# Attention scan with an MLP on one core: one sum moved from VectorE to matmuls, mask copies moved from GpSimd, and a new order of steps

## The chip, the cores and the metric

The kernel runs on one core of one Trainium2 chip. The metric is the device time of one execution in microseconds (us), taken outside the profiler; three runs of the kernel before gave 550.18, 550.34 and 550.40 us, median 550.34.

## What is computed

A gated linear attention with a complex decay, and a two-layer MLP on its output. The decay is normalised first; the change touches the magnitude in it.

```python
B, H, S, D = 4, 8, 768, 48
mag = np.sqrt(a_re * a_re + a_im * a_im)
scale = np.minimum(mag, 0.999) / (mag + 1e-06)
a_re_n, a_im_n = (a_re * scale, a_im * scale)
for t in range(S):
    new_re = ar * S_re - ai * S_im
    new_im = ar * S_im + ai * S_re
    S_re, S_im = (new_re + k_t v_t^T, new_im)
    y[t] = q_t @ S_re
...
h = x @ w_in            # 3072 x 384 by 384 x 2048
out = (h * sigmoid(1.702 * h)) @ w_out
```

## The kernel before

The 3072 tokens are cut into 12 units of 256 tokens. A unit has two chunks of 128 tokens, and unit 0 is prepared in two parts of 128 tokens. Units form groups: unit 0 alone, unit 1 alone, then pairs. For each unit three things happen:

- `prepare_part` (L298 on) turns the decay into factors for q and k: squares on ScalarE (L207), their sum on VectorE (`both("sum", ...)`, helper line L231), logarithm, root and reciprocal on ScalarE (L331 to L336), products and scans over time on VectorE (L358, L378, and L398 for the angle), sine and cosine on ScalarE (L421 to L427; L406 turns the angle into a count of turns), the products with q and k on VectorE (L231), and DMAs that rearrange them by head (`remap`, L452 to L456).
- `attend` (L460 on) makes scores on TensorE (L517), masks them on VectorE (L523), transposes keys (L536, copied out as `kt` by ScalarE, L542), sums scores and state into `x_ps` (L507, copied out at L567), and makes the new state in `z_ps` (L561, "state matmuls" below).
- `moe` (L625 on) multiplies by the weights: `h_ps` (L657), the activation on ScalarE (L665, L669, L671), `o_ps` (L686). Group 0 uses the weights whole, in float32; the groups after it use them split in a high and a low part. The weights come as 64-bit floats and are turned to 32-bit ones by three VectorE steps and one ScalarE step for each 768 columns (`convert`: L249, L252, L255, L256).

Each step is put down by `plan.add` with its engine and with keys that it reads and writes. A table of numbers, `ORDER`, then lists all steps; they are issued in that order, so each engine and the SP queue of DMAs run theirs in the table's order, each engine in order of its own queue.

TensorE begins with 20 "filler" matmuls (L434, `WARM = 20`), products with the identity whose result nobody reads. Ahead of the table stand constants: the identity, a causal mask in four rotated forms (one made by memset and affine_select, three more by 12 copies of 32 rows by 128 columns on GpSimd, L160), and zeroed state tiles.

The core of what is edited:

```python
both("sum", u, i, rk("sum"), d, m, d, ALU.add, r=k_mag, w=k_den)
...
add("ACT", a_t(C), rk("root"), lambda: act(out=m, in_=d, func=AF.Ln, bias=b_tiny), r=k_den, w=k_mag, ...)
...
nc.gpsimd.tensor_copy(out=mask[o * QL : (o + 1) * QL, j, :], in_=mask[g * QL : (g + 1) * QL, 0, :])
```

Of the kernel before, what the change touches and what calls it, by code (L numbers as in the profile page):

```python
# [95 lines left out]
def attention_moe(ctx: ExitStack, tc: tile.TileContext, qk_in, v, a_in, w_in, w_out, qn, kn, vn, an, bn, out):  # L96
# [49 lines left out]
    nc.vector.memset(b_hpi, HALF_PI)  # L146
    make_identity(nc, ident)
    nc.gpsimd.memset(mask, 1.0)
    nc.gpsimd.memset(runs, 1)
    run_of = {T: runs[:, 0 : NR * (T + 1)], L: runs[:, NR * (T + 1) :]}  # L150
    for n, x in run_of.items():
        nc.gpsimd.memset(x.rearrange("p (r t) -> p r t", t=n + 1)[:, :, 0], 0)
    nc.gpsimd.affine_select(
        out=mask[:, 0, :], in_=mask[:, 0, :], pattern=[[1, P]], compare_op=ALU.is_ge,
        fill=0.0, base=0, channel_multiplier=-1,
    )
    for j in range(1, 4):
        for g in range(4):
            o = (g + j) % 4
            nc.gpsimd.tensor_copy(out=mask[o * QL : (o + 1) * QL, j, :], in_=mask[g * QL : (g + 1) * QL, 0, :])  # L160
# [65 lines left out]
    def both(op, u, i, rank, out, a, b, alu, **kw):  # L226
        n = 1
        for x in out.shape[1:]:
            n *= x
        e, en, t = two(on(op, u, i), n)  # L230
        add(en, t, rank, lambda: e.tensor_tensor(out=out, in0=a, in1=b, op=alu), **kw)  # L231
# [66 lines left out]
    def prepare_part(u, i, a, b, np_, mag, den, rec, sp, th, *keys):  # L298
# [31 lines left out]
        both("sum", u, i, rk("sum"), d, m, d, ALU.add, r=k_mag, w=k_den)  # L330
        add("ACT", a_t(C), rk("logd"), lambda: act(out=g, in_=m, func=AF.Ln, bias=b_tiny), r=k_mag, w=k_sp, tab=LOGS, grp=u or None)  # L331
        add("ACT", a_t(C) - 0.1, rk("logd"), lambda: act(out=g, in_=g, func=AF.Exp, scale=-0.5), w=k_sp, tab=LOGS, grp=u or None)
        add("ACT", a_t(C), rk("root"), lambda: act(out=m, in_=d, func=AF.Ln, bias=b_tiny), r=k_den, w=k_mag, tab=LOGS, grp=u or None)
# [430 lines left out]
    for g, us in enumerate(GROUPS):  # L764
        for u in us:
            prepare(u)
            attend(u)
        moe(g)
        if g == 0:
            for n in range(2 * NP):  # L770
                split(n)
# [375 lines left out]
```

## Time and profile before

| what | value |
|---|---|
| median of 3 runs | 550.34 us |
| the profiled execution's own time | 550.39 us |
| its span, first to last instruction | 548.7 us |
| TensorE busy | 521.2 us, 95% |
| VectorE busy | 391.1 us, 71% |
| ScalarE busy | 368.7 us, 67% |
| GpSimd busy | 12.3 us, 2% |
| granted TensorE clock | 1.00 |

The profiled execution took 0.05 us more than the median, and 1.69 us of it lie outside the span. Busy shares are averages: VectorE is full in the first fifth of the span and a quarter full at the end, while TensorE starts late and is then busy to the end. In a timeline row "start us, us" is a merged stretch of like instructions, xN their count; a float32 matmul leaves two records. On VectorE and ScalarE the listed time of an instruction is longer than the distance to the next one's start where the two overlap, so what an instruction costs its queue is read from the starts.

### The profile page before, as it was taken

Reading aid. Unit: us, or ns where it says so; the run is one execution under the profiler, and the core shown is the slowest. Engines: PE = TensorE matmul, PEld = TensorE weight load, DVE = VectorE, ACT = ScalarE, POOL = GpSimd, SP = SyncE. Lnnn points to the kernel's source line nnn. Section 1 sums busy time; section 2 is a strip of 40 time slices with the busy share of each in tenths; the row PEclk is TensorE's granted clock in tenths of the full one; section 3 lists DMA queues with packets and bytes.
Section 4 is the critical chain, followed back from the end, with each engine's and each line's share of the span. In section 5 each row is a group of like instructions: output and inputs, shape, how many; then the busy total and the mean of one; then the engine's idle time right before and its main releaser. Section 6 shows DMA issues by size and latency. Waiting matters only on the chain.

```text
span 548.7 us, 14354 instructions
## 1 busy us (share of the span) xinstructions
PE 521.2 (95%) x6122; PEld 446.9 (81%) x6122; DVE 391.1 (71%) x625; ACT 368.7 (67%) x559; POOL 12.3 (2%) x55
## 2 busy tenths in 40 slices
PE   0399999999999999999999999999999999999997
PEld 0389988999988888888888888888888888888885
DVE  7999999999979989987766844856366535421142
ACT  7898989979699988688795679248665242132221
POOL 7000000000000000000000000000000000000000
PEclk9999999999999999999999999999999999999999
DMA  8859963626576668868237427445441162100121
GB/s 344 284 191 354 252 258 89 206 54 156 201 181 202 151 197 206 236 168 252 74 92 228 68 65 174 145 133 117 136 134 49 50 145 91 62 15 34 39 87 61
DMA packets 29253, 82.02 MB, mean 149 GB/s; under 512 B 4096, under 2 KB 7168, under 8 KB 29184
## 3 DMA queue, kind: packets, MB, share of 16 engines
q1 hardware_dynamic: 29184, 81.06, 50.5%
q8 instruction: 49, 0.80, 0.6%
q14 instruction: 20, 0.16, 0.1%
HBM read 57.41 MB, written 4.72 MB: 113 GB/s over the span
## 4 chain that ended last, share of the span: by engine, by line
PE 89%; DVE 8%; DMA 1%; issue 1%; ACT 1%; SPq 0%; DVEq 0%
PE o_ps L686 36%; PE h_ps L657 36%; PE x_ps L507 7%; PE z_ps L561 3%; PE z_ps L517 3%; PE p_ps L517 2%; DVE qk L231 1%; PE p_ps L536 1%; PE z_ps L536 1%; DMA raw<-in_w_in_dram 1%; DVE s L231 1%; DVE valA L256 1%; DVE qr L231 1%; DVE valU L252 0%; DMA qkh<-qk 0%
## 5 line engine op out<-in xcount | busy, mean ns | idle before, releaser
L669 ACT ACTIVATE gh<-h_ps 128x512 fp32r<-128x512 f32 x88 | 52.4, 596 | 108.2 <-PE h_ps L657 76.5
L673 DVE TENSOR_TENSOR gl<-h_ps,gh 128x512 fp32r<-128x512 f32 x88 | 60.3, 687 | 85.3 <-ACT h_ps L671 74.0
L657 PE MATMUL h_ps<-xhi,hiA 128*128 128x512 f32 (+1 forms) x288 | 108.9, 378 | 0.4 <-DVE gl L673 0.4
L657 PE MATMUL h_ps<-xhi,loA 128*128 128x512 f32 (+1 forms) x288 | 107.1, 372 | 0.0
L657 PE MATMUL h_ps<-xlo,hiA 128*128 128x512 f32 (+1 forms) x288 | 107.0, 372 | 0.0
L686 PE MATMUL o_ps<-gh,hiU 128*128 128x512 f32 (+1 forms) x288 | 79.7, 377 | 0.0
L686 PE MATMUL o_ps<-gl,hiU 128*128 128x512 f32 (+1 forms) x288 | 79.4, 376 | 0.0
L686 PE MATMUL o_ps<-gh,loU 128*128 128x512 f32 (+1 forms) x288 | 78.2, 372 | 0.0
L890 ACT ACT_TABLE_LOAD x56 | 71.8, 1283 | 1.8 <-PEq L1135 0.9
L657 PEld LDWEIGHTS h_ps<-xhi,hiA 128*128 128x128 f32 x288 | 54.2, 188 | 10.6 <-DVE gl L673 0.9
L657 PEld LDWEIGHTS h_ps<-xhi,loA 128*128 128x128 f32 x288 | 54.2, 188 | 9.6
L657 PEld LDWEIGHTS h_ps<-xlo,hiA 128*128 128x128 f32 x288 | 54.3, 188 | 9.0
L686 PEld LDWEIGHTS o_ps<-gh,loU 128*128 128x128 f32 x288 | 52.3, 188 | 9.5
L686 PEld LDWEIGHTS o_ps<-gh,hiU 128*128 128x128 f32 x288 | 51.4, 188 | 9.9 <-ACT gh L669 0.5
L686 PEld LDWEIGHTS o_ps<-gl,hiU 128*128 128x128 f32 x288 | 51.5, 188 | 9.6 <-issue 0.4
L671 ACT ACTIVATE h_ps<-h_ps 128x512 f32<-128x512 f32 x88 | 51.8, 592 | 0.0
L231 DVE TENSOR_TENSOR qk<-qk,s 128x768 f32<-128x768 f32 (+2 forms) x39 | 44.0, 1134 | 0.8 <-ACT s L427 0.5
L507 PE MATMUL x_ps<-pm,v 128*32 128x128 f32 x768 | 39.4, 274 | 0.0
L723 DVE TENSOR_REDUCE fit<-raw_w 128x1 f32<-128x384 f32 x64 | 33.5, 544 | 5.4 <-DMA raw_w<-in_w_out_dram 4.4
L507 PE MATMUL x_ps<-qkh,st 96*32 96x128 f32 x640 | 34.0, 272 | 0.0
L434 PE MATMUL h_ps<-qk,ident 128*128 128x256 f32 x40 | 11.9, 460 | 22.2 <-DVE qk L231 22.2
L434 PEld LDWEIGHTS h_ps<-qk,ident 128*128 128x128 f32 x40 | 9.2, 237 | 23.8 <-issue 22.2
(104 smaller groups left out, 791.2 us busy)
## 6 DMA issues: line engine op xcount, KB each, us to landing
v<-in_v_dram SPq DMA_DIRECT2D x24, 416.0 KB, 4.4
ri<-in_a_dram SPq DMA_DIRECT2D x11, 768.0 KB, 5.9
qk<-in_qk_dram SPq DMA_DIRECT2D x11, 768.0 KB, 6.4
qkh<-qr SPq DMA_DIRECT2D x22, 288.6 KB, 5.8
qkh<-qk SPq DMA_DIRECT2D x22, 288.6 KB, 4.8
raw<-in_w_in_dram SPq DMA_DIRECT2D x8, 768.0 KB, 7.1
raw<-in_w_out_dram SPq DMA_DIRECT2D x8, 768.0 KB, 7.4
raw_w<-in_w_in_dram SPq DMA_DIRECT2D x16, 384.0 KB, 3.3
```

The costliest lines, as they stand in the source:

```text
L231: add(en, t, rank, lambda: e.tensor_tensor(out=out, in0=a, in1=b, op=alu), **kw)
L434: add("PE", 0.43, -WARM + k, lambda k=k, dst=dst: mm(h_ps[0][:, k % 2 * T : (k % 2 + 1) * T], lhsT=ident, rhs=dst[:, k % NR, 0:T], start=T ...
L507: mm(x_ps[32 * j : 32 * j + 32, r, :], lhsT=lt, rhs=rt, start=n == 0, stop=n == len(steps) - 1)
L517: mm(ps_[to : to + QL, j, lo:L], lhsT=at(h, 1, c)[:, lo : lo + QL], rhs=at(h, 0, c)[:, lo:L], start=True, stop=True)
L561: mm(z_ps[g * QL : (g + 1) * QL, h * D : h * D + D], lhsT=kt[h // 4][:, h % 4, g * QL : (g + 1) * QL], rhs=vt[:, lo : lo + D], start=True, ...
L657: mm(h_ps[hb][:, k * n_x : (k + 1) * n_x], lhsT=ww[:, r * T + f * P : r * T + (f + 1) * P], rhs=x[:, r, xs], start=n == 0, stop=n == last)
L669: add("ACT", a_t(CW) - 0.13, rk(order_), lambda hb=hb, gb=gb: act(out=high.g(gb), in_=h_ps[hb], func=AF.Silu, scale=SLOPE), r=[f"h{hb}"], ...
L671: add("ACT", a_t(CW) - 0.13, rk(order_), lambda hb=hb: act(out=h_ps[hb], in_=h_ps[hb], func=AF.Silu, scale=SLOPE), w=[f"h{hb}"], tab=SILU, ...
L673: add("DVE", d_t(CW), rk(order_), lambda hb=hb, gb=gb: dve.tensor_tensor(out=glo[gb], in0=h_ps[hb], in1=high.g(gb).bitcast(F32), op=ALU.su ...
L686: mm(o_ps[c][:, xs], lhsT=y[:, f * DM + c * P : f * DM + (c + 1) * P], rhs=x[:, k * n_x : (k + 1) * n_x], start=begins and k == 0 and n == ...
L723: add("DVE", d_t(CK), rk + 2, lambda x=x, op=op: dve.tensor_reduce(out=f_w[:, x, n : n + 1], in_=weights.looked_at()[:, :, 1], op=op, axis ...
L890: nc.scalar.preload_act_table_set(o[5])
```

## The change

The sum of squares of unit 1 goes by six matmuls with the identity, which add the two squares in PSUM (`h_ps[1]` and `o_ps[2]`); the logarithm after it reads PSUM in two pieces. The 12 mask copies are issued to VectorE; the memset of the mask covers one form only. `prepare(1)` is put down before `moe(0)`, and `ORDER` has 1737 steps in place of 1736, nearly all in new places.

```diff
+    nc.gpsimd.memset(mask[:, 0, :], 1.0)
+    nc.gpsimd.affine_select(
+        out=mask[:, 0, :], in_=mask[:, 0, :], pattern=[[1, P]], compare_op=ALU.is_ge,
+        fill=0.0, base=0, channel_multiplier=-1,
+    )
     make_identity(nc, ident)
-    nc.gpsimd.memset(mask, 1.0)
...
-            nc.gpsimd.tensor_copy(out=mask[o * QL : (o + 1) * QL, j, :], in_=mask[g * QL : (g + 1) * QL, 0, :])
+            nc.vector.tensor_copy(out=mask[o * QL : (o + 1) * QL, j, :], in_=mask[g * QL : (g + 1) * QL, 0, :])
...
-        both("sum", u, i, rk("sum"), d, m, d, ALU.add, r=k_mag, w=k_den)
+        roots = [(d, m, k_den)]
+        if u == 1:
+            roots = [(h_ps[1].rearrange("p (r t) -> p r t", r=2), m[:, 0:2, :], ["h1"]), (o_ps[2][:, 0:T], m[:, 2, :], ["o2"])]
+
+            def total():
+                for r in range(NR):
+                    for x in (m, d):
+                        mm(roots[r // 2][0][:, r, :] if r < 2 else roots[1][0], lhsT=ident, rhs=x[:, r, :], start=x is m, stop=x is d)
+
+            add("PE", 2.6, rk("sum"), total, r=k_mag + k_den, w=["h1", "o2"])
+        else:
+            both("sum", u, i, rk("sum"), d, m, d, ALU.add, r=k_mag, w=k_den)
...
-        add("ACT", a_t(C), rk("root"), lambda: act(out=m, in_=d, func=AF.Ln, bias=b_tiny), r=k_den, w=k_mag, tab=LOGS, grp=u or None)
+        for sums, to, ks_ in roots:
+            add("ACT", a_t(C // len(roots)), rk("root"), lambda sums=sums, to=to: act(out=to, in_=sums, func=AF.Ln, bias=b_tiny),
+                r=ks_, w=k_mag, tab=LOGS, grp=u or None)
...
         for u in us:
-            prepare(u)
+            if u != 1:
+                prepare(u)
             attend(u)
+        if g == 0:
+            prepare(1)
         moe(g)
...
-80 0 137 5 15 20 100 25 81 82 84 83 85 86 1 3 2 87 94 139 4 138 88 103
```

In the new file the lines of `prepare_part` behind the edit, of `attend` and of `moe` have numbers that are 12 or 13 higher (L345 for L333, L419 for L406, L530 for L517, L555 for L542, L574 for L561, L670 for L657).

VectorE's queue at the start, from its first product on; before:

```order
L231 TENSOR_TENSOR s_84<-s_83,s_84 128x3x128
L249 TENSOR_SCALAR valA_159<-raw_72 128x768
L252 SCALAR_TENSOR_TENSOR valA_159<-raw_72,valA_159 128x768
L231 TENSOR_TENSOR s_84<-ri,s_86 128x3x128
L256 ISA valA_159<-raw_72,valA_159 128x1536
L231 TENSOR_TENSOR s_84<-s_83,s_84 128x3x128
L249 TENSOR_SCALAR valA_173<-raw_73 128x768
L339 TENSOR_SCALAR s_83<-s_83 128x3x128
L252 SCALAR_TENSOR_TENSOR valA_173<-raw_73,valA_173 128x768
L358 SCALAR_TENSOR_TENSOR s_86<-s_83,s_85 128x129 x3
```

And with the change:

```order
L231 TENSOR_TENSOR s_84<-s_83,s_84 128x3x128
L249 TENSOR_SCALAR valU_160<-raw_76 128x768
L252 SCALAR_TENSOR_TENSOR valU_160<-raw_76,valU_160 128x768
L231 TENSOR_TENSOR s_84<-ri,s_86 128x3x128
L160 COPY mask<-mask 32x128 x12
L352 TENSOR_SCALAR s_83<-s_83 128x3x128
L231 TENSOR_TENSOR s_84<-s_83,s_84 128x3x128
L249 TENSOR_SCALAR valA_175<-raw_73 128x768
L371 SCALAR_TENSOR_TENSOR s_86<-s_83,s_85 128x129 x3
```

The 12 copies stand ahead of the scan of unit 0's first part, and two conversion steps (L256, L252) that stood there went behind it.

TensorE's queue between the first scores of unit 0 and its first state matmuls, with the change (L447 are the fillers, L337 the new sums):

```order
L549 MATMUL o_ps_110<-ident,qkh_78 128x96 x4
L549 MATMUL o_ps_109<-ident,qkh_78 128x96 x4
L337 MATMUL h_ps_108<-s_86,ident 128x256
L337 MATMUL h_ps_108<-s_84,ident 128x256
L337 MATMUL o_ps_111<-s_86,ident 128x256
L337 MATMUL o_ps_111<-s_84,ident 128x256
L447 MATMUL h_ps_107<-qk,ident 128x256 x7
L574 MATMUL z_ps<-v_88,kt_99 32x48 x12
```

Before, 5 and 2 fillers stood around the second transposes there; now six sums and 7 fillers stand ahead of the state matmuls.

ScalarE's queue around the copies of the transposed keys (`kt`) of unit 0's second chunk; before:

```order
L218 ACTIVATE s_85<-s_85 128x3x256
L890 ACT_TABLE_LOAD
L353 ACTIVATE s_84<-s_84 128x3x256
L542 ACTIVATE kt_100<-z_ps 128x384
L370 ACTIVATE fit<-s_83 128x3
L542 ACTIVATE kt_99<-p_ps 128x384
L890 ACT_TABLE_LOAD
L665 ACTIVATE g_499<-h_ps_107 128x512
L406 ACTIVATE s_84<-s_87 128x3x256
```

And with the change:

```order
L218 ACTIVATE s_85<-s_85 128x3x256
L906 ACT_TABLE_LOAD
L366 ACTIVATE s_84<-s_84 128x3x256
L255 ACTIVATE raw_76<-raw_76 128x768
L555 ACTIVATE kt_100<-z_ps 128x384
L419 ACTIVATE s_84<-s_87 128x3x256
L383 ACTIVATE fit<-s_83 128x3
L555 ACTIVATE kt_99<-p_ps 128x384
L906 ACT_TABLE_LOAD
L678 ACTIVATE g_559<-h_ps_107 128x512
```

The turns of unit 1 (L406, now L419) moved from behind both copies to between them; that instruction reads the angle scan of unit 1 on VectorE.

## Rows read from the trace of the kernel before

**Rows 1.** The page: busy time of TensorE, its share of the span, instructions.

```profile
PE 521.2 (95%) x6122; PEld 446.9 (81%) x6122; DVE 391.1 (71%) x625; ACT 368.7 (67%) x559; POOL 12.3 (2%) x55
```

**Rows 2.** Waits of TensorE: who waited for whom, total us, times, longest.

```profile
PE h_ps L434 <- DVE qk L231: 22.2, 1, 22.2
PE z_ps L561 <- DVE pm L523: 0.8, 1, 0.8
```

**Rows 3.** Timeline of TensorE, 22 to 50 us: start, length, line, tiles, records.

```profile
22.21 8.38 PE L434 MATMUL h_ps<-qk,ident 128*128 128x256 f32 x26 [22.21 <-DVE qk L231]
...
37.45 0.84 PE L561 MATMUL z_ps<-v,kt 128*32 128x48 f32 x46 [0.78 <-DVE pm L523]
...
39.92 2.94 PE L657 MATMUL h_ps<-x,valA 128*128 128x128 f32 x24
...
45.49 0.42 PE L507 MATMUL x_ps<-pm,v 128*32 128x128 f32 x8
...
47.39 0.94 PE L686 MATMUL o_ps<-g,valU 128*128 128x128 f32 x6
...
48.93 0.88 PE L561 MATMUL z_ps<-v,kt 128*32 128x48 f32 x48
49.74 1.60 PE L686 MATMUL o_ps<-g,valU 128*128 128x128 f32 x12
```

**Rows 4.** Timeline of VectorE, 7.5 to 24 us.

```profile
9.75 0.65 DVE L249 TENSOR_SCALAR valA<-raw 128x768 int32<-128x768 int32 x1
10.32 0.77 DVE L339 TENSOR_SCALAR s<-s 128x384 f32<-128x384 f32 x1
...
13.29 0.15 DVE L366 TENSOR_SCALAR small<-s 128x3 f32<-128x3 f32 x1
13.48 0.18 DVE L367 RECIPROCAL small<-small 128x3 f32<-128x3 f32 x1
13.57 0.53 DVE L249 TENSOR_SCALAR valA<-raw 128x768 int32<-128x768 int32 x1
14.02 0.42 DVE L339 TENSOR_SCALAR s<-s 128x384 f32<-128x384 f32 x1
...
18.20 0.95 DVE L252 SCALAR_TENSOR_TENSOR valU<-raw,valU 128x768 int32<-128x768 int32 x1
19.07 0.16 DVE L417 TENSOR_SCALAR s<-s 128x3 f32<-128x3 f32 x1
19.14 1.05 DVE L358 TENSOR_TENSOR_SCAN s<-s,s 128x129 f32<-128x129 f32 x3
```

**Rows 5.** Timeline of GpSimd: the mask copies.

```profile
3.64 6.34 POOL L160 COPY mask<-mask 32x128 bf16<-32x128 bf16 x12
```

**Rows 6.** Timeline of VectorE, 40 to 46 us: the scans of unit 1.

```profile
41.62 1.88 DVE L358 TENSOR_TENSOR_SCAN s<-s,s 128x257 f32<-128x257 f32 x3
...
43.84 1.78 DVE L398 TENSOR_TENSOR_SCAN s<-runs,s 128x771 f32<-128x771 uint8 x1
```

**Rows 7.** Timeline of ScalarE: second key copy of chunk 1, and the turns of unit 1.

```profile
44.04 0.48 ACT L542 ACTIVATE kt<-p_ps 128x384 f32<-128x384 f32 x1
...
46.33 0.83 ACT L406 ACTIVATE s<-s 128x768 int32<-128x768 f32 x1
```

**Rows 8.** Timeline of TensorE, 130 to 135 us: attention between two stretches of the MLP.

```profile
130.31 0.52 PE L686 MATMUL o_ps<-gh,loU 128*128 128x256 f32 x3
130.67 0.52 PE L686 MATMUL o_ps<-gl,hiU 128*128 128x256 f32 x3
131.12 0.42 PE L507 MATMUL x_ps<-pm,v 128*32 128x128 f32 x8
...
133.80 0.41 PE L507 MATMUL x_ps<-qkh,st 96*32 96x128 f32 x8
134.14 0.39 PE L657 MATMUL h_ps<-xhi,hiA 128*128 128x256 f32 x1
134.36 0.28 PE L657 MATMUL h_ps<-xlo,hiA 128*128 128x256 f32 x1
```

More of the change, by code (lines that the diff above doesn't have):

```diff
@@ L152, in attention_moe @@
         nc.gpsimd.memset(x.rearrange("p (r t) -> p r t", t=n + 1)[:, :, 0], 0)
[L153 to L156, printed above, removed]
     for j in range(1, 4):
```

145 rows, old and new, of the table ORDER are left out of this document.

## The prediction

> **What bounds the kernel now.** I read the page first: TensorE is busy for 95% of the span [rows 1]. Its list of waits says where the other 5% lie: 22.2 us ahead of the first matmul, 0.8 us at the first state matmuls [rows 2], and the tail behind the last matmul, whose steps the new order leaves as they are. So the time is the start, plus the work of TensorE, plus what TensorE loses on the way. Its timeline shows where the loss stops [rows 3]: from 22.21 it runs fillers, with scores, transposes and waits between them; from the first MLP matmul at 39.92 the stretches follow each other almost without a hole. Later than that, a change can only add or save waits or passages from one kind of matmul to another. Ahead of that VectorE decides: it has hardly an idle moment from 5 us on, and the first filler itself was released by it [rows 2]. VectorE's timeline gives what each instruction costs its queue [rows 4, 6], GpSimd's the mask copies [rows 5], ScalarE's the place of the key copies [rows 7].
>
> **The start on VectorE.** Ahead of the product that releases TensorE the new order has two L252 less (0.87 us each, from 18.20 to 19.07), one L339 less (about 0.35) and one scan of three pieces less (about 1.0, listed 1.05) [rows 4]: 3.1 us less. While GpSimd copied masks (6.34 us in all [rows 5]) VectorE was slower: L339 took 0.77 us at 10.32 and 0.42 at 14.02, L249 0.65 at 9.75 and 0.53 at 13.57 [rows 4]; with three more like the second I estimate 0.7 us that come back. Against this stand the 12 copies. No row shows a copy of 32 x 128 on VectorE. A three-column operation lets the next start 0.07 us later (19.07 to 19.14), a 768-column one 0.45 us later (13.57 to 14.02) [rows 4]; on a line between them 128 columns cost 0.13 us, 12 copies 1.6 us. The lower end is 12 x 0.07 = 0.8. The upper end is a copy that starts only when the one before has finished: 0.19 us as from 13.29 to 13.48 [rows 4], plus 0.06 for the columns, 12 x 0.25 = 3.0. I take 1.6, because the copies read one form and write the others, so none needs the result of the one before, while the step at 13.48 does need it. The first filler then starts 3.1 + 0.7 - 1.6 = 2.2 us earlier, at 20.0.
>
> A rule of the Trainium skill speaks for the upper end: in "VectorE: DVE Perf Modes", section "Two Vector instructions with no wait between them", an instruction whose input or output begins in another group of 32 partitions than that of the one before is held until all earlier ones have finished. No row here shows such a pair. Each of these copies changes both groups, so by that rule the copies would cost the 3.0 us of the upper end, and the sum below would be 552.1 where by the line between the two rows it is 550.7; it is the first rival.
>
> **The sums on TensorE.** Six matmuls leave 12 records of 256 columns. A record of 128 columns in float32 takes 2.94/24 = 0.12 us [rows 3], so twice the columns take 0.245 and the six sums 2.9 us; the fillers' mean, 8.38/26 = 0.32 [rows 3], would make it 3.9. They stand ahead of the first state matmuls, in the time in which TensorE ran fillers and waited before: no cost by itself. But TensorE runs in order, so the sums and the seven fillers behind them (14 x 0.245 = 3.4) hold back the state matmuls. From 20.0 its own queue is: 13 fillers 8.4 [rows 3], scores and transposes of the first chunk about 2.0, sums 2.9, fillers 3.4, state matmuls 0.8, `x_ps` 0.7, scores of the second chunk 1.2 (the small ones are estimates): 39.4 for the first MLP matmul, against 39.92 [rows 3]. The wait of 0.8 us [rows 2] goes: the masked scores and key copies are ready by then.
>
> **What is late next.** From 39.92 to 45.49 TensorE did 42 records of MLP and two sets of transposes [rows 3], 5.6 us; the new order puts the same work there, so from 39.4 it would come to the state matmuls of chunk 1 at 45.0. These need both copies of the transposed keys. Before, the second started at 44.04, ahead of the turns of unit 1 (46.33) [rows 7]. Now the turns stand between the two copies, and behind them wait the second key copy, the table load and the first activation of the MLP. The turns need the angle scan of unit 1. The scan ahead of that started at 41.62 [rows 6]. In front of it VectorE now has one L249 (0.45), one L252 (0.87) and the sum of unit 1 (768 columns of two sources, as L252, 0.87) less, 2.2 us, and 0.7 less of slowing, and 1.6 more of copies: 40.3. Then that scan, listed 1.88, and the angle scan, listed 1.78 [rows 6], about 0.1 less each to the next start: 43.8. The turns take 0.83, the copy 0.48 [rows 7], so with some waking the state matmuls start at about 45.2 and TensorE waits 0.2 us. State matmuls take 0.81 (48.93 to 49.74), `x_ps` 1.90 (45.49 to 47.39) [rows 3]: the first projection matmul starts at 47.9. Before it started at 47.39, with the 0.81 us of state matmuls still ahead [rows 3]; for equal work that is 47.1. **Gain 0.3 us.** By the copies' lower end TensorE's own queue decides at 45.0, a gain of 0.5; by the upper end it is a loss of 1.1.
>
> **The rest of the order.** After this TensorE is full in both, with the same multiplications. What differs is how often attention matmuls interrupt the MLP: counting in the two orders, TensorE goes from scores, `x_ps` or state matmuls to MLP matmuls 29 times before and 31 times now. What a passage costs: three records take 0.36 (130.31 to 130.67), and the next kind starts 0.45 later (131.12), 0.09 lost; on the way back the first record takes 0.22 where 0.12 is usual (134.14 to 134.36), 0.1 lost, and about 0.1 more lies in the 0.34 ahead of it [rows 8]. Two more at 0.3 us make **0.6 us of loss**. At least it is nothing (passages that coincide with waits), at most twice that. One table load of ScalarE less is worth nothing, since TensorE does not wait for ScalarE there.
>
> Sum: 550.39 - 0.3 + 0.6 = 550.7 us against the profiled execution's own 550.39, which is 0.05 above the median. Within 0.2% of the median, 549.2 to 551.4, is about what a measurement of this kernel can't tell from no change. So: **no change, 550.7 us.**
>
> **The rivals.**
> - *The copies are held, and the key copy is late (slower).* Place: the turns of unit 1 ahead of the second key copy. Each 0.1 us on a copy moves the angle scan, the key copy and so TensorE by 1.2 us. With 3.0 us for the copies the time is 550.7 + 1.4 = 552.1. It decides from 0.19 us a copy on (2.3 us in all, 551.4). For it: the change of partitions in every copy, and VectorE without a gap from the copies to the scan. Against it: the copies don't need each other. Chance 0.22; another 0.08 for a weight conversion that comes late behind the work of unit 1, which the new order pulls ahead of conversions, at about the same time.
> - *TensorE's queue runs without a wait (faster).* If copies cost 0.8 and 0.9 us of slowing come back instead of 0.7, TensorE's queue and VectorE's scans both stand 1.0 us earlier than I count; the state matmuls then start at 44.2 and, for equal work, the first projection at 46.1, a gain of 1.3, and if the passages fall into waits and cost nothing more the time is 550.39 - 1.3 = 549.1. For it: VectorE and GpSimd no longer disturb each other. Against it: it takes the ends of two estimates, and a full ScalarE queue that follows. Chance 0.2.
>
> **How the numbers follow.** Forecast 0.5, slower 0.3, faster 0.2. The forecast's own range is 549.9 to 551.4 (gain of 0.5 and no passages lost, to copies near 0.19); with the rivals' middles the range is 549.1 to 552.1, and what lies beyond it I put at 2 in 10.
>
> **What would show it.** First filler near 20.0; copies 0.13 us apart; first MLP matmul near 39.4; state matmuls of chunk 1 near 45.2 after a wait of some 0.2 us that is put down to the key copy; first projection at 47.9; the last matmul 0.3 us later than before. I am wrong if copies lie 0.19 us apart or more, if TensorE's waits behind 48 us grow by more than 0.5 us, or if the state matmuls don't wait at all.

## The result and the profile after

The changed kernel takes 553.05 us (median of 5, 552.91 to 553.40) against 550.23 for the kernel before (5 runs): a ratio of 1.0051, 95% interval [1.0039, 1.0064]. It is slower by 2.8 us, above the range of the forecast, which ended at 552.1. The profiled execution took 552.91 us, 2.5 more than that of before.

The page of the changed kernel, its first line and TensorE's line:

```profile
span 551.1 us, 14383 instructions
PE 524.4 (95%) x6134; PEld 449.1 (81%) x6134; DVE 391.2 (71%) x636; ACT 367.0 (67%) x559; POOL 5.2 (1%) x43
```

TensorE is as full as before [rows 1], GpSimd's copies are gone, and the span is 2.4 us longer. TensorE's waits (us in total, times, longest):

```profile
PE h_ps L447 <- DVE qk L231: 21.0, 1, 21.0
PE o_ps L699 <- ACT gh L682: 0.9, 1, 0.9
PE z_ps L574 <- ACT kt L555: 0.6, 1, 0.6
```

The start is 1.2 us shorter than in [rows 2] and the wait of 0.8 at the first state matmuls is gone; two new waits, both for ScalarE, stand in its place. A third wait of the kernel before, at 106 us, is gone too; [rows 2] leave it out:

```profile
PE h_ps L657 <- DVE gl L673: 0.4, 1, 0.4
```

TensorE's timeline from the start to the first projection, which is the first `o_ps` matmul of the MLP, L699 (start, length of the stretch, what, count of records), which answers to [rows 3]:

```profile
21.00 8.14 PE L447 MATMUL h_ps<-qk,ident 128*128 128x256 f32 x26 [21.00 <-DVE qk L231]
...
31.20 1.92 PE L337 MATMUL h_ps<-s,ident 128*128 128x256 f32 x8
32.95 1.03 PE L337 MATMUL o_ps<-s,ident 128*128 128x256 f32 x4
33.82 3.18 PE L447 MATMUL h_ps<-qk,ident 128*128 128x256 f32 x14
36.93 0.84 PE L574 MATMUL z_ps<-v,kt 128*32 128x48 f32 x45
...
39.91 1.60 PE L670 MATMUL h_ps<-x,valA 128*128 128x128 f32 x12
...
46.13 0.84 PE L574 MATMUL z_ps<-v,kt 128*32 128x48 f32 x45 [0.58 <-ACT kt L555]
...
48.88 0.94 PE L699 MATMUL o_ps<-g,valU 128*128 128x128 f32 x6
```

The sums take 33.82 - 31.20 = 2.62 us. The first MLP matmul comes at 39.91, where it was at 39.92. The first projection comes at 48.88; before, at 47.39 with 0.81 us of state matmuls still ahead, so at 48.20 for equal work. **By then 0.68 us are lost.** The last two records, after and before:

```profile
546.81 0.19 PE L774 MATMUL p_ps<-small 128*1 128x1 f32 x2
```

```profile
544.40 0.19 PE L761 MATMUL p_ps<-small 128*1 128x1 f32 x2
```

The second of the two starts 0.03 us after the first, at 546.84 and, before, at 544.43, so the rest takes 497.96 instead of 496.23: **1.73 us more are lost behind the first projection.** The two losses make the 2.4 us of the span.

VectorE's timeline at the copies and at the product that releases TensorE ([rows 4] before):

```profile
8.16 2.37 DVE L160 COPY mask<-mask 32x128 bf16<-32x128 bf16 x12
...
19.94 0.95 DVE L231 TENSOR_TENSOR qk<-qk,s 128x768 f32<-128x768 f32 x1
```

With the next instruction at 10.57 the copies cost 2.4 us, 0.20 each; GpSimd took 6.34 for them [rows 5]. ScalarE's timeline at the start of the MLP ([rows 7] before):

```profile
38.17 0.47 ACT L594 ACTIVATE st<-z_ps 96x384 f32<-96x384 f32 x1
...
39.28 0.47 ACT L580 ACTIVATE x<-x_ps 128x384 f32<-128x384 f32 x1
...
44.77 0.84 ACT L419 ACTIVATE s<-s 128x768 int32<-128x768 f32 x1 [0.94 <-DVE s L411]
45.52 0.19 ACT L383 ACTIVATE fit<-s 128x3 f32<-128x3 f32 x1
45.61 0.47 ACT L555 ACTIVATE kt<-p_ps 128x384 f32<-128x384 f32 x1
```

From 29.22 to 43.34 ScalarE has no gap worth a name, and its copy of `x` at 39.28 ends as TensorE gets to the MLP. The turns (L419) wait 0.94 us for the angle scan and hold the key copy to 45.61. ScalarE and TensorE at the late wait:

```profile
242.42 1.28 ACT L906 ACT_TABLE_LOAD   x1
...
247.25 1.28 ACT L906 ACT_TABLE_LOAD   x1
248.54 0.85 ACT L440 ACTIVATE s<-s 128x768 f32<-128x768 f32 x1
249.29 0.58 ACT L682 ACTIVATE gh<-h_ps 128x512 fp32r<-128x512 f32 x1
```

```profile
248.23 0.84 PE L699 MATMUL o_ps<-gl,hiU 128*128 128x512 f32 x3
249.93 0.96 PE L699 MATMUL o_ps<-gh,hiU 128*128 128x512 f32 x3 [0.86 <-ACT gh L682]
```

TensorE has used up the activations it had when ScalarE is still behind four logarithm and exponential steps, two table loads and a sine step (L440).

### The profile page after: what moved, and what is told of

The parts are those of the page before. It is cut to its first block, busy times and chain, and to the rows that moved or that the text cites. A ratio compares the mean times of both kernels' runs of the same rounds, so it can differ in the third digit from the quotient of the medians.

```text
span 551.1 us, 14383 instructions
## 1 busy us (share of the span) xinstructions
PE 524.4 (95%) x6134; PEld 449.1 (81%) x6134; DVE 391.2 (71%) x636; ACT 367.0 (67%) x559; POOL 5.2 (1%) x43
## 4 chain that ended last, share of the span: by engine, by line
PE 77%; DVE 8%; ACT 8%; issue 2%; DVEq 0%; ACTq 0%
PE o_ps L699 32%; PE h_ps L670 31%; PE x_ps L520 6%; PE z_ps L574 2%; PE p_ps L530 2%; PE z_ps L530 2%; ACT L906 2%; DVE qk L231 1%; DVE qr L231 1%; PE p_ps L549 1%; PE z_ps L549 1%; DVE s L371 1%; ACT s L342 1%; ACT s L345 1%; DVE s L391 1%
## 5 line engine op out<-in xcount | busy, mean ns | idle before, releaser
L670 PE MATMUL h_ps<-xhi,hiA 128*128 128x512 f32 (+1 forms) x288 | 108.5, 377 | 0.0
L670 PE MATMUL h_ps<-xhi,loA 128*128 128x512 f32 (+1 forms) x288 | 107.1, 372 | 0.0
L670 PE MATMUL h_ps<-xlo,hiA 128*128 128x512 f32 (+1 forms) x288 | 107.1, 372 | 0.0
L699 PE MATMUL o_ps<-gh,hiU 128*128 128x512 f32 (+1 forms) x288 | 80.1, 378 | 0.9 <-ACT gh L682 0.9
L699 PE MATMUL o_ps<-gl,hiU 128*128 128x512 f32 (+1 forms) x288 | 79.9, 378 | 0.1
L699 PE MATMUL o_ps<-gh,loU 128*128 128x512 f32 (+1 forms) x288 | 78.2, 372 | 0.0
L670 PEld LDWEIGHTS h_ps<-xhi,hiA 128*128 128x128 f32 x288 | 54.2, 188 | 9.8 <-DVE gl L686 0.3
L670 PEld LDWEIGHTS h_ps<-xhi,loA 128*128 128x128 f32 x288 | 54.2, 188 | 9.6
L670 PEld LDWEIGHTS h_ps<-xlo,hiA 128*128 128x128 f32 x288 | 54.3, 188 | 9.1
L699 PEld LDWEIGHTS o_ps<-gh,loU 128*128 128x128 f32 x288 | 52.2, 188 | 9.6
L699 PEld LDWEIGHTS o_ps<-gh,hiU 128*128 128x128 f32 x288 | 51.1, 188 | 10.9 <-ACT gh L682 1.3
L699 PEld LDWEIGHTS o_ps<-gl,hiU 128*128 128x128 f32 x288 | 51.3, 188 | 10.2 <-DVE gl L686 0.9
L447 PE MATMUL h_ps<-qk,ident 128*128 128x256 f32 x40 | 11.3, 449 | 21.0 <-DVE qk L231 21.0
L447 PEld LDWEIGHTS h_ps<-qk,ident 128*128 128x128 f32 x40 | 9.2, 232 | 22.6 <-issue 21.0
```

The lines of the kernel that those rows point to most:

```text
L447: add("PE", 0.43, -WARM + k, lambda k=k, dst=dst: mm(h_ps[0][:, k % 2 * T : (k % 2 + 1) * T], lhsT=ident, rhs=dst[:, k % NR, 0:T], start=T ...
L670: mm(h_ps[hb][:, k * n_x : (k + 1) * n_x], lhsT=ww[:, r * T + f * P : r * T + (f + 1) * P], rhs=x[:, r, xs], start=n == 0, stop=n == last)
L699: mm(o_ps[c][:, xs], lhsT=y[:, f * DM + c * P : f * DM + (c + 1) * P], rhs=x[:, k * n_x : (k + 1) * n_x], start=begins and k == 0 and n == ...
```

## The experiments

The theory: VectorE pays for the copies because they stand in the middle of its full queue, the lateness reaches TensorE at the start, and the new order adds the late wait. Rivals: the order alone costs the time; the late key copy alone costs it; the sums cost it. Times of before that stand beside the runs lie between 550.20 and 550.41. The intervals of most of these runs are 1.0 to 1.5 us wide, so a difference of half a microsecond between two of them rests on the rows of their traces and not on the times. In kernels where the copies are issued by the loop that issues the table, line numbers are 4 lower.

### The mask part alone, in the old order (`mask_only`)

```diff
-            nc.gpsimd.tensor_copy(out=mask[o * QL : (o + 1) * QL, j, :], in_=mask[g * QL : (g + 1) * QL, 0, :])
+            nc.vector.tensor_copy(out=mask[o * QL : (o + 1) * QL, j, :], in_=mask[g * QL : (g + 1) * QL, 0, :])
```

> The kernel before and its order, with the mask part of the change alone (triangle made first, 12 block copies on VectorE). Theory 'held copies': the copies lie 0.20 us apart as in the changed kernel, 2.4 us in all, and 0.7 us of slowing by GpSimd comes back, so the first filler starts at 22.2 + 1.7 = 23.9. TensorE had 0.8 us of wait behind it to take that up, so the time is 0.9 to 1.7 above the kernel before: 551.1 to 551.9. Rival 'the copies are covered, the order alone costs the time': first filler by 22.9 and 550.2 within 0.5.

552.07 us, ratio 1.0029 [1.0018, 1.0041], just above what was expected. TensorE's first row, its first state matmuls and its first MLP matmuls:

```profile
23.97 8.65 PE L434 MATMUL h_ps<-qk,ident 128*128 128x256 f32 x26 [23.97 <-DVE qk L231]
...
39.16 0.84 PE L561 MATMUL z_ps<-v,kt 128*32 128x48 f32 x46 [0.46 <-DVE pm L523]
...
41.62 2.94 PE L657 MATMUL h_ps<-x,valA 128*128 128x128 f32 x24
```

The first filler comes 1.76 us later than in [rows 3]. The wait for the masked scores takes up only 0.3 of that (0.46 instead of 0.78), the fillers take about as much longer (8.65 instead of 8.38), and the time is 1.75 us above that of before. The rival falls: in the order of before, with no other change, the copies cost 1.75 us.

### The changed kernel with the copies on GpSimd (`pool_copies`)

> The changed kernel and its order, with the 12 block copies back on GpSimd. Theory 'held copies, then the key copy late': VectorE gets 2.4 us back and loses some 0.7 to GpSimd's copies, first filler at 19.3 instead of 21.0, the angle scan of unit 1 at 41.3 instead of 42.97, TensorE's wait of 0.58 us for the key copy is gone and the state matmuls of chunk 1 start 0.6 to 1.7 earlier: 551.3 to 552.4. Rival 'the order alone costs the time': 553.0 within 0.4, and the wait stands.

551.67 us, ratio 1.0023 [1.0014, 1.0033]: 1.4 us below the changed kernel, 1.4 above the one before, and inside what was expected. TensorE's first row, the state matmuls of chunk 1 and the first projection:

```profile
19.19 7.42 PE L447 MATMUL h_ps<-qk,ident 128*128 128x256 f32 x26 [19.19 <-DVE qk L231]
...
44.28 0.84 PE L574 MATMUL z_ps<-v,kt 128*32 128x48 f32 x45 [0.67 <-ACT kt L555]
...
47.03 0.94 PE L699 MATMUL o_ps<-g,valU 128*128 128x128 f32 x6
```

The first filler is near the 19.3 that was expected. The wait for the key copy is not gone: VectorE, ScalarE and TensorE all come 1.85 us earlier at this place and keep their distances. So both have a part, the copies and the new order. The profiled execution took 552.82, more than the median, with a wait of 1.4 us at 358 us that the changed kernel does not have; it stays unexplained.

### Why a copy takes 0.20 us (`copies_twice`, `halves`)

Both stand on the kernel of the next section. `copies_twice` issues each copy two times in a row:

> As the run with the copies in VectorE's first gap, but each copy is issued twice in a row, so that of 24 copies every second one has the partitions of the one before. Theory 'a copy is held where its partitions change': the second of a pair starts 0.07 to 0.13 us after the first, the first of the next pair 0.19 to 0.20 after the second. Rival 'a copy of this size takes 0.20 wherever it stands': 0.20 throughout. The first filler at 18.8 plus 0.8 to 1.6 by the one, plus 2.4 by the other.

The copies start 0.22 us apart within a pair and 0.20 from pair to pair. By the words of the expectation this is the rival's case, but it decides nothing: the second of a pair writes the cells of the first and waits on a semaphore for it. `halves` has no such waits:

```diff
-                nc.vector.tensor_copy(out=mask[o * QL : (o + 1) * QL, j, :], in_=mask[g * QL : (g + 1) * QL, 0, :])
+                for c in (slice(0, 64), slice(64, 128)):
+                    nc.vector.tensor_copy(out=mask[o * QL : (o + 1) * QL, j, c], in_=mask[g * QL : (g + 1) * QL, 0, c])
```

> As the run with the copies in VectorE's first gap, but each block copy is issued as two of 64 columns, with the same partitions, other columns and no wait between them. Theory 'held where the partitions change': the second half starts 0.07 to 0.12 us after the first, the first half of the next block 0.17 to 0.20 after the second half. Rival 'any copy this short takes its whole length before the next starts': the same distance, 0.16 to 0.20, within a pair and between pairs. Behind the first one, which ends when GpSimd's memsets do (3.8 us).

VectorE's group of all 24 (shortest, median and longest in ns, first and last start), then its timeline in two windows, 3.9 to 4.1 and 4.1 to 4.2, each with two copies merged:

```profile
L903 DVE COPY mask<-mask x24: 162/170/1008, 2.8 to 6.7; 32x64 bf16<-32x64 bf16 x24
```

```profile
3.84 0.26 DVE L903 COPY mask<-mask 32x64 bf16<-32x64 bf16 x2
3.94 0.35 DVE L903 COPY mask<-mask 32x64 bf16<-32x64 bf16 x2
```

One copy lasts 0.17. Two halves of the same block cover 0.26 us, so the second starts 0.09 after the first, before it has ended. A second half and the first half of the next block cover 0.35, twice 0.17: the next one starts when the other has ended, 0.18 later. Same length, same size, no wait in either; only the partitions differ. That is the held rule which the prediction set against its own line between two rows (the Trainium skill, "VectorE: DVE Perf Modes", section "Two Vector instructions with no wait between them"): the trace agrees with the rule. The rival is out.

### The copies in VectorE's first gap (`copies_early`)

VectorE had nothing to do from 2.78 to 5.01 us, and the triangle is ready by 1.5. In the changed kernel the copies come after four planned steps. Here they are issued first:

```diff
+        for j in range(1, 4):
+            for g in range(4):
+                o = (g + j) % 4
+                nc.vector.tensor_copy(out=mask[o * QL : (o + 1) * QL, j, :], in_=mask[g * QL : (g + 1) * QL, 0, :])
         for n in order:
```

> The changed kernel; the 12 block copies stay on VectorE but stand ahead of its first planned step (the square sum at 5.01 us), in the time from 2.78 to 5.01 in which VectorE waited, instead of behind four planned steps at 8.16. Theory 'what counts is where the copies stand': they take the same 2.4 us, 0.2 of it beyond the gap, the first filler starts at 21.0 - 2.4 + 0.2 = 18.8 and the time is 1.4 to 2.2 below the changed kernel: 550.9 to 551.7. Rival 'the time is set behind 48 us, an earlier start is taken back by later waits': 552.4 or more.

552.59 us, ratio 1.0042 [1.0028, 1.0055]: by the time alone the rival's case. But the start is not as early as the theory had it. The first filler is at 20.07 instead of 18.8, the first projection at 47.92, 0.96 earlier than in the changed kernel; half of that shows in the median here (the intervals overlap), and all of it in the pair with the old order behind (`early_old_tail` against `old_tail`, 551.85 - 550.82 = 1.0). VectorE's copies, and GpSimd's last memset:

```profile
2.80 3.21 DVE L902 COPY mask<-mask 32x128 bf16<-32x128 bf16 x12
```

```profile
3.67 0.10 POOL L351 MEMSET s<- 128x3 f32 x1
```

The first copy alone lasted 1.02 us, to 3.82; GpSimd's memsets ended at 3.77, and from the second on the copies lie 0.20 apart. So 12 copies took 3.2 us here, and VectorE's first product came 1.03 us late, at 6.04. The Trainium skill ("SBUF — State Buffer", section "Who interferes with whom") has a port pair that VectorE, in its two-port modes, shares with GpSimd; whoever issues first holds it for the whole instruction while the other waits. The row agrees that the copy waits, though not for one instruction: it lasts until the last of a chain of memsets. No run here moves the memsets, so the cause rests on the two ends, 3.82 and 3.77.

### The key copy and the turns (`key_copy_first`, `turns_later`)

One number of the table moved, the second key copy ahead of the turns; then, in the second run, the turns and the VectorE step that reads them behind the first activation of the MLP as well.

> The changed kernel with one step moved: the second copy of the transposed keys of chunk 1 stands ahead of the turns of unit 1 on ScalarE. Theory 'the key copy is late': the copy starts at 43.8 instead of 45.6, TensorE's wait of 0.58 us is gone, state matmuls at 45.5, time 552.4 to 552.6. Rival 'the loss moves on': the turns start 0.5 later, and unit 1's chain or the first MLP activation holds TensorE by the same 0.5: 552.9 to 553.2.

552.90 us, ratio 1.0045 [1.0031, 1.0059], as the rival had it. The wait for the key copy is gone, and TensorE waits 0.51 us for the first activation, which stands behind the turns and a table load:

```profile
48.34 0.82 PE L699 MATMUL o_ps<-g,valU 128*128 128x128 f32 x5 [0.51 <-ACT g L678]
```

> The changed kernel with the turns of unit 1 (and the one VectorE step that reads them) moved behind the first activation of the MLP on ScalarE, so that the order there is key copy, table load, activation, turns, as before the change. Theory 'the turns delay two things, the key copy and the activation': both waits (0.6 at the state matmuls, 0.5 at the first projection when only the key copy was moved) are gone, first projection at 48.0 to 48.1 instead of 48.88, time 552.2 to 552.5. Rival 'the later turns delay unit 1 and a later wait takes it back': 552.8 to 553.3.

553.42 us, ratio 1.0056 [1.0042, 1.0069]. That is a little above the rival's range. Neither wait is there, and TensorE waits 0.4 us for an activation at 57.0 us. But the first projection comes only at 48.70, where 48.0 to 48.1 was expected: in this trace the fillers ended 0.64 us later than in the changed kernel (last section). How much of the missing gain is that and how much the later wait is not separated. In both runs the time goes the rival's way: with the wait for the key copy gone, the gain is 0.15 us at most. The late key copy alone does not cost the time.

### The sums (`old_order`, `sum_back`, `seven_less`)

`old_order` keeps all edits and puts the steps in the order of before.

> All edits of the change (copies on VectorE, sum of unit 1 by matmuls), but the steps in the order of before; the six sum matmuls stand where the addition stood, ahead of the second scores, and the fillers as before. Theory 'copies at the start, new order behind': the copies cost 0.9 to 1.7 as alone, the sums 2.6 us on TensorE's queue against 0.8 us of wait there, both overlap in part, so the first MLP matmul comes 1.8 to 2.7 later than 39.92; the second wait for a weight-to-output activation (1.0 us, at 248 us in the changed kernel) and the two more passages are not there: 552.0 to 552.9. Rival 'the new order gains more at the start than it loses later': above 553.4.

554.23 us, ratio 1.0066 [1.0053, 1.0080], above what was expected: 2.2 us more than the mask part alone in the same order. The six matmuls stand ahead of the second scores, and the first MLP matmul comes at 43.14 instead of 41.62:

```profile
43.14 2.94 PE L670 MATMUL h_ps<-x,valA 128*128 128x128 f32 x24
```

This is the range of the rival: with all edits in place, the new order gains more at the start than it loses later. With the new order up to step 525 alone the time is 551.85 (`old_tail`, below), with all of it 553.05; so of the 2.4 us that its first part gains its second part gives back 1.2. `sum_back` keeps the new order and gives the sum back to VectorE:

```diff
-        if u == 1:
+        if u < 0:
```

> The changed kernel and its order, with the sum of unit 1 as one addition on VectorE again, in the place of the six matmuls; one activation takes the root instead of two. Theory 'in the new order the matmuls are free and the addition is not': TensorE has 2.6 us less to do in a stretch where it would wait for ScalarE anyway, VectorE 0.87 more ahead of the angle scan, so turns, key copy and state matmuls come up to 0.87 later: 553.4 to 553.9. Rival 'the matmuls cost in the new order as in the old, where they cost 2.1': 551.0 to 552.4.

554.63 us, ratio 1.0081 [1.0068, 1.0095]: 1.6 us more than with the matmuls. The sign is the theory's, the size, above the expected 553.9, is not. VectorE is 1.0 us later at the angle scan (44.01 instead of 42.97); and TensorE, which waited 2.4 us between 36 and 41 us (1.73 for ScalarE's state copy, 0.71 for a DMA), came back slower. The windows (length, then busy time and count of PE, PEld, DVE, ACT, POOL, then the granted clock):

```profile
36.00:41.00 5.00, 2.56 (x75) 2.15 (x65) 5.00 (x7) 4.92 (x8) 0.10 (x1) 0.86 0.40 108
41.00:43.40 2.40, 2.40 (x14) 2.40 (x14) 2.40 (x5) 2.28 (x3) 0.10 (x1) 0.58 1.01 375
```

The granted clock is 0.58 from 41.0 to 43.4, most of it the lower level of 1.2 GHz, and the 12 records of the first MLP matmuls take 2.56 us where the changed kernel's take 1.60. So some 1.0 us of the difference in this trace is the lower clock and not the addition's own time. `seven_less` leaves out the seven fillers behind the sums, whose result nobody reads.

> The changed kernel without the seven filler matmuls behind the sums (3.2 us of TensorE from 33.82 on; they are no part of the result). Theory 'ScalarE sets the first MLP matmul': its queue from 29.1 to 44 us has no gap and brings the copy of x at 39.28 whatever TensorE does, so the first MLP matmul stays at 39.7 to 40.0, TensorE waits some 3 us ahead of it, and the time stays at 553.0 within 0.4. Rival 'the sums and fillers hold TensorE back': first MLP matmul at 36.8 to 38.5 and 550.5 to 552.0.

554.31 us, ratio 1.0076 [1.0062, 1.0089]. The place is the theory's, the time is neither's:

```profile
38.70 1.08 PE L530 MATMUL z_ps<-qkh 96*32 96x128 f32 x32 [2.74 <-ACT st L594]
39.81 1.60 PE L670 MATMUL h_ps<-x,valA 128*128 128x128 f32 x12
```

With 3.2 us less to do TensorE waits 2.74 for ScalarE, and the first MLP matmul stays at 39.81: here ScalarE sets it. In the changed kernel, where TensorE comes to it without a wait at 39.91, its own queue and ScalarE stand within 0.1 us of each other. Why the run is 1.3 us longer than the changed kernel is open. The profiled execution has a second wait for an activation, 0.97 us long with its restart, at 161 us; its clock reads 1.00. The two timed runs with the lowest clock, 0.994, are the longest, 554.97 and 555.46, so a lower clock is a part of it in these.

### The late order (`old_tail`, `gh_first`)

`old_tail` keeps the first 525 steps of the new table and has the others in the order of before; the cut lies in front of the late wait.

> The changed kernel with its first 525 of 1737 steps in the new order and the rest in the order of before. Theory 'the new order loses 1.7 us behind 100 us' (from the first projection to the last matmul 497.96 us in the changed kernel, 496.23 for equal work in the one before): the wait of 1.0 us at 248 us and the 0.23 at 298 are gone, the passages fewer by two: 551.2 to 551.7. Rival 'the late wait comes from the later start of the long units, whatever the order': 552.8 to 553.3.

551.85 us, ratio 1.0028 [1.0015, 1.0040]: 1.2 us below the changed kernel, a little above what was expected. From the first projection (48.84) to the last matmul (545.95) it takes 497.11 us, 0.85 less than the changed kernel. The wait at 248 us is gone; the waits behind TensorE's first:

```profile
PE z_ps L574 <- ACT kt L555: 0.7, 1, 0.7
PE z_ps L530 <- issue: 0.3, 1, 0.3
```

`gh_first` keeps the new order and moves one step, the sine step L440, behind the two activations:

> The changed kernel with one step moved: on ScalarE at 248.5 us the 0.85 us sine step goes behind the two activations of the MLP that TensorE waits for. Theory 'ScalarE's order there makes the wait': the wait of 1.0 us at 248 us falls to 0.2 to 0.3 and the time by 0.7 to 0.8, 552.2 to 552.4. Rival 'the loss moves on': the step moved is late for the next unit, another wait grows, 552.8 to 553.2.

552.43 us, ratio 1.0040 [1.0026, 1.0054], 0.6 less than the changed kernel and within 0.05 of what was expected. ScalarE there, then TensorE:

```profile
248.45 0.60 ACT L682 ACTIVATE gh<-h_ps 128x512 fp32r<-128x512 f32 x1
248.94 0.59 ACT L684 ACTIVATE h_ps<-h_ps 128x512 f32<-128x512 f32 x1
249.46 0.84 ACT L440 ACTIVATE s<-s 128x768 f32<-128x768 f32 x1
```

```profile
248.12 0.84 PE L699 MATMUL o_ps<-gl,hiU 128*128 128x512 f32 x3
249.10 0.96 PE L699 MATMUL o_ps<-gh,hiU 128*128 128x512 f32 x3
```

The activation comes 0.84 earlier. Between these two groups TensorE's starts lie 0.98 us apart, where 0.68 is usual: 0.30 too long instead of 1.02 (248.23 to 249.93 in the changed kernel). This gain was not taken back, as the theory had it. The intervals of this run and of the changed kernel overlap, though each of its five executions is shorter than each of the changed kernel's; the wait in the trace is what settles it: ScalarE's order at one place makes it.

### Versions meant to beat both kernels

`split_before`: the kernel before with six copies on ScalarE in its gap from 2.17 us and six on VectorE in its own. `early_old_tail`, `split_copies`, `split_old_tail`, `split_gh`: the changed kernel with the copies early or so split, and one of the late repairs.

> The kernel before and its order, with the mask part alone and the copies spread over two gaps, six on ScalarE from 2.17 us, six on VectorE until 5.0. Theory 'the copies cost where they stand': no copy delays a planned step and GpSimd no longer slows VectorE (some 0.7 us), so the first filler starts at 21.4 to 22.2 instead of 22.21, and the time is 549.5 to 550.3, up to 0.8 below the kernel before. Rival 'the mask part costs wherever it is put': 551.0 to 552.0.

> Both edits of the two runs before: copies in VectorE's first gap, and from step 526 on the order of before. If the two losses are independent they add: 553.05 - 1.4 to 2.2 - 1.4 to 1.7, so 549.2 to 550.2, at or below the kernel before. If either stands in for the other, 550.6 or more.

> A version to beat both kernels: six of the block copies on ScalarE in its gap from 2.17 to 4.04, six on VectorE in its gap until 5.01; the turns of unit 1 behind the first MLP activation; steps from 526 on in the order of before. If the three losses add (copies 2.4 of which some 2.0 reach the end, key copy and activation 0.6, late order 1.2): first filler at 18.5 to 19.0, first projection at 45.6 to 46.5, 549.2 (548.6 to 550.0). Rival 'another bound stands close behind': 550.3 or more.

> As the combined version run before, without the moved turns: copies spread over the two gaps, old order from step 526 on. With the moved turns it was 550.55, and the moved turns alone added 0.4 to the changed kernel: 550.0 to 550.5 if that holds here. Rival 'the turns were worth their place once VectorE is earlier': 550.6 to 551.2.

> The changed kernel and its order with two edits: copies spread over the two gaps (six on ScalarE, six on VectorE) and the sine step at 248.5 us behind the two activations. If both add (copies 1.4 to 2.0, by the run with the copies on GpSimd and by VectorE's 2.4; the sine step 0.6): 550.4 to 551.1. Rival 'the later waits close the gap': 551.5 or more.

| run | us | ratio to before, interval |
|---|---|---|
| split_before | 550.50 | 1.0005 [0.9996, 1.0014] |
| split_copies | 550.55 | 1.0006 [0.9997, 1.0015] |
| split_old_tail | 550.53 | 1.0004 [0.9995, 1.0013] |
| early_old_tail | 550.82 | 1.0009 [1.0000, 1.0018] |
| split_gh | 551.06 | 1.0013 [1.0004, 1.0022] |

None beats the kernel before. `split_before` shows what it was for: spread over two gaps the same copies cost nothing that can be measured, where they cost 1.75 us in the middle of VectorE's full stretch. They gain nothing either, though the first filler comes 0.26 us earlier (21.95) and a gain of up to 0.8 was thought possible. `split_gh` against `gh_first` gives their price in the new order, 552.43 - 551.06 = 1.4 us. Only `split_gh` came out inside its expectation; the four others lie above theirs, `split_before` and `split_old_tail` by 0.2 us or less, `early_old_tail` by 0.6, in part since its first copy too waited for GpSimd, and `split_copies` by 0.5, with the moved turns bringing nothing here as before. By their times these two belong to the alternatives that they named (550.6 or more, 550.3 or more): something else stands close behind, and what it is was not tested. The profiled execution of `split_copies` (552.64 us, median 550.55) had its first load late, on ScalarE:

```profile
5.22 0.94 ACT L203 ACTIVATE s<-ri 128x384 f32<-128x384 f32 x2 [1.21 <-DMA ri<-in_a_dram]
```

The other profiled executions have this row between 4.04 and 4.46, so such an execution says little about the edit.

## Why the prediction was wrong

**The copies: the step that failed at the start.** "I take 1.6, because the copies read one form and write the others, so none needs the result of the one before." They don't need it and are held all the same: 2.4 us. The point from which the first rival was to decide, 0.19 us a copy, was reached: 0.8 us more on VectorE than forecast, and the first filler at 21.00 instead of 20.0. The gain of 0.3 by the first projection became a loss of 0.68. The distance from 13.29 to 13.48 [rows 4], which was set aside as that of a step that needs the one before, was the nearer one. The other 0.2 us of the first filler lies in the terms beside the copies. The slowing by GpSimd was one: the differences that the prediction lists for it add up to 0.8, it took 0.7, and `mask_only` gives 0.6 (22.21 + 2.4 - 23.97).

**"After this TensorE is full in both": the step that failed behind.** Only passages were counted there, 0.6 us, and ScalarE was put at nothing, "since TensorE does not wait for ScalarE there". What came is 1.73, with one wait of 0.86 us for ScalarE's activation. TensorE's interval there was 1.02 too long, of which `gh_first` gave 0.6 us back; the old order from there on gave 1.2. The new order of ScalarE was looked at where the change begins and not where it goes on. What is left of the 1.73 is not assigned: some 0.5 us by the time of the run with the old order, 0.9 by its trace. The new order also saves the wait of 0.4 us at 106 us, which the prediction's list of TensorE's waits leaves out, so there is that much more to assign than the balance shows. A part of it may be the passages.

**Right in size, with a second bound unseen.** The first MLP matmul was forecast at 39.4 from TensorE's own queue and came at 39.91. TensorE did come to it without a wait, but `seven_less` shows that ScalarE's state copy and copy of `x` would hold it at 39.8 anyway. Fewer fillers could have made it earlier by 0.1 us at most; a longer queue makes it later, as in `turns_later` (40.55, last section).

**Right in kind, not worth its length.** The state matmuls wait for the key copy behind the turns, 0.58 us instead of 0.2, as the rival had it. But to take the wait away brought 0.15 us at most, since the next thing in ScalarE's queue was late by as much.

**Right.** The sums: 2.62 us against 2.9, and in the new order they stand where TensorE would wait for ScalarE if it had less to do (`seven_less`). With the sum on VectorE the time there is 1.6 us longer, a part of it by the lower clock; in the old order the edits beside the copies cost 2.2. The wait of 0.8 us goes. GpSimd's slowing of VectorE is real: in VectorE's rows of `pool_copies` instructions at 5 to 8 us again take 0.63 to 0.68 us where the changed kernel's take 0.55.

## What to carry to other kernels

Ask of a moved instruction first where it lands in its new queue: the same 12 copies cost 1.4 to 1.75 us in the middle of a full queue and nothing that can be measured when spread over the gaps of two engines 5 us earlier. All 12 in VectorE's gap were too long for it by 1.0 us, mostly since the first waited. When a whole order is new, read every engine that feeds the full one along its whole length, and look for a run of table loads and long steps ahead of something the full engine reads. Of a wait of 0.58 us that was taken away ahead of a full ScalarE, 0.51 came back at the next thing that it feeds.

## What was not expected of the hardware

- Short VectorE copies: 0.09 us from start to start where the partitions stay, 0.18 where they change (32 x 64), 0.20 for 32 x 128.
- A VectorE copy issued at 2.80 us lasted until GpSimd's memsets were over: 1.02 us instead of 0.19.
- TensorE's first records run at half the rate for a time that differs between executions, while the granted clock reads 1.00. The windows of the fillers (columns as above), first of the changed kernel, then of `old_tail`, which has the same first steps; between 24 and 26 us it has 10 records where the changed kernel has 7:

```profile
24.00:26.00 2.00, 2.00 (x7) 1.59 (x7) 1.97 (x8) 2.00 (x5) 0.00 (x0) 1.00 0.23 52
26.00:28.00 2.00, 2.00 (x11) 1.77 (x10) 1.97 (x4) 1.91 (x3) 0.00 (x0) 1.00 0.40 66
```

```profile
24.00:26.00 2.00, 2.00 (x10) 1.71 (x10) 1.97 (x8) 2.00 (x5) 0.00 (x0) 1.00 0.23 51
```

Records lie 0.43 us apart and then 0.22; of the 26, between 6 and 13 lie the longer distance apart in the executions here. In the old order a wait behind the fillers takes this up in part: it is 0.78 us in the kernel before [rows 3], where the fillers take 8.38, and 0.46 in `mask_only`, where they take 8.65. In the new order no such wait is left: `turns_later` began its fillers at 20.96, ended them 0.64 us later than the changed kernel (29.70, 29.06), and came to its first MLP matmul at 40.55. How much of the spread between executions of one kernel comes from this was not tested.
